# One core, attention and two expert layers: the buffers of the splits, the order of the first loads, and the place of the weight pieces in VectorE's queue

## The chip, the cores and the metric

The kernel runs on one core of a Trainium2 chip. The core has TensorE (PE in the profile, with its weight loads as PEld), VectorE (DVE), ScalarE (ACT), GpSimd (POOL) and SyncE (SP), which issues most of the DMAs. The metric is the device time of one execution in microseconds.

## What is computed

Three layers in a row, on 4 sequences of 576 positions:

```python
# 1: attention, 8 heads of 64, causal by blocks of 64
scores = where(mask, q @ k.T / 8, -1e9)
x = softmax(scores) @ v                       # (4, 576, 512) after joining heads
# 2: a dense layer
xn = (x - mean(x)) / sqrt(var(x) + 1e-6) * g_ln
x = x + relu(xn @ w_ch1) @ w_ch2              # 512 -> 2048 -> 512
# 3: one of 8 experts for each token, chosen by the gate of this token
#    or taken over from the token before
out[b, s] = p[e] * (relu(x[b, s] @ w1[e]) @ w2[e])   # 512 -> 1024 -> 512
```

All inputs are float32; the results are wanted at float32 accuracy.

## The kernel before

**Tiles and steps.** The 2304 tokens are 18 tiles of 128. Attention goes through 144 steps, one for a tile and a head, in the order of the tiles. Matrix products run in float16: each operand is split into a high part and the rest (three matmuls in place of one). A step is: scores (`qk`, PE), row maxima (`maxes`, DVE, L328 and L332), exponentials (`exps`, ACT L339), their split (ACT L348, POOL L351), a transposing DMA issued by SP (L355), and some steps later the product with the values (`pv`, PE L370 and L374).

**Splits of a tile.** Before a tile's steps its keys and queries are cast to float16 (`split_k`, `split_q`: ACT L245 and L230), the rest is subtracted (POOL, for the first tile DVE: L246 and L231), and a transposing DMA brings them into the layout that `qk` reads (SP L247 and L237); DVE makes a copy of the queries with halves exchanged (L238, L239). The values are split without a transpose (`split_v`). A tile's splits are written one tile ahead, at heads `SK`, `SQ` and `SV` of the tile before; its loads are written two tiles ahead.

**End of a tile.** `finish` normalises the attention's result; its normalised rows `xh` are cast, subtracted and transposed (ACT L422, POOL L423, SP L427). `xh`, the keys' `kn` and the queries' `qn` are requests of one ring of three buffers, the tag `nat`, handed out in the order in which the code asks.

**Weights of the dense layer.** They come as 32 pieces of 512 KB (16 of `w_ch1`, 16 of `w_ch2`), read as whole numbers of 64 bits would be and put together again by three DVE passes in `w_bits` (L195, L199, L202; L199 and L202 read two inputs in SBUF). Then ACT scales and casts (`w_hi`: L215, L216) and POOL subtracts (`w_lo`, L220). `w_next` takes one step in this chain: bits of piece p, the high part of p-1 and the load of p+2 (three raw buffers), the rest of p-2. `WPACE[s]` says how many such steps are written at attention step s.

**Dense work.** When a tile (or a group of tiles) is finished, its first layer (16 pieces `l1`, 12 matmuls each, evicted by ACT L477 and DVE L478) and its second layer (4 pieces `l2` a tile, L495 to L497) go into a queue. At each step some are written, as many as a running account allows, and only those whose weights have been written: `need(q) <= wpos - 3`, where `wpos` counts the `w_next` steps so far; a first-layer piece f needs weight piece 4*(f//4)+3, a second-layer piece c needs 16+4*c+3.

**Order.** A scheduler puts the instructions into the engines' queues. It goes by the order of the code, except that instructions written inside `tc.high_priority(HP)` come 400 places earlier; an instruction whose inputs are ready may pass one that is not. `first(i)` gives this precedence to steps of tiles i < `HT`. Everything up to attention step 0 is written in order by hand: `PRE` lists the first loads, `FIRST` the first splits and weight steps (an integer loads that weight piece, "k" loads keys, "K" splits them, "w" is one `w_next`).

**Late buffers.** From step `LATE` on the raw weight buffers are given back, and the rings of scores (`sm`), split exponentials (`ph`) and transposed ones (`pt`) get 1, 2 and 1 more buffers; `pv` then lags 5 steps in place of 4.

Of the kernel before, what the change touches and what calls it, by code (L numbers as in the profile page):

```python
# [10 lines left out]
F16 = mybir.dt.float16  # L11
# [38 lines left out]
LAG = 4  # L50
LATE = 32
MSM = 1
# [8 lines left out]
SK = 3  # L61
# [3 lines left out]
PK = 4  # L65
PRE = (0, "k", "q", 1, "v", 2)
FIRST = ("w", "K", "Q", "w", "V", "w")
RB = 4
ACAP = 20000
FREE = 16  # L70
HP = 400
HT = 2
MAN = 0
# [8 lines left out]
PUMP = (5, 1, 1, 4, 12, 4)  # L82
WPACE = [0]*2+[2]*16


@with_exitstack
def kernel(
# [139 lines left out]
    def split_q(i, eng):  # L227
        r = raw.pop(("q", i))
        n = at.tile([P, H, 2, D], F16, tag="nat", name="qn", bufs=3)
        nc.scalar.copy(out=n[:, :, 0], in_=r)  # L230
        eng.tensor_tensor(out=n[:, :, 1], in0=r, in1=n[:, :, 0], op=ALU.subtract)  # L231
        o = (KRING + VRING + turn_q[0] % 2 * 2) * 1024
        turn_q[0] += 1
        a, b = (
            spare[:, x:x + 1024].rearrange("p (h c) -> p h c", h=H) for x in (o, o + 1024)
        )
        nc.sync.dma_start_transpose(out=a, in_=n.rearrange("p h e d -> p (h e d)"))  # L237
        nc.vector.tensor_copy(b[0:D], a[D:P])  # L238
        nc.vector.tensor_copy(b[D:P], a[0:D])  # L239
        qt[i, 0], qt[i, 1] = a, b  # L240

    def split_k(i, eng):
        r = raw.pop(("k", i))
        n = at.tile([P, H, 2, D], F16, tag="nat", name="kn", bufs=3)
        nc.scalar.copy(out=n[:, :, 0], in_=r)  # L245
# [71 lines left out]
    def maxes(i, h):  # L317
# [7 lines left out]
        if h == 0:  # L325
            sums[i] = at.tile([P, 2, H], F32, tag="sums", name="sums", bufs=2)
        nm = sums[i][:, 0, h:h + 1]
        nc.vector.tensor_tensor_reduce(  # L328
            out=sm[:, lo:n], in0=sp[:, lo:n], in1=mask[:, 5 * P - n + lo:5 * P],
# [62 lines left out]
    def finish(i):  # L392
# [27 lines left out]
        )  # L420
        xh = at.tile([P, 2, DM], F16, tag="nat", name="xh", bufs=3)
        nc.scalar.copy(out=xh[:, 0], in_=xn)  # L422
# [239 lines left out]

    wpos = [0]


    def w_next(n=1):
        for _ in range(n):
            p = wpos[0]
            wpos[0] += 1
            if p < 32:  # L670
                w_bits(p)
# [48 lines left out]
    def first(i):  # L720
        return tc.high_priority(HP) if i < HT else ExitStack()
# [15 lines left out]
    for s in range(nsteps + LAG + MPT):  # L737
# [8 lines left out]
        if s < nsteps:  # L746
# [9 lines left out]
            if t + 1 < NTILE:  # L756
                nx = ORDER[t + 1]
                if h == SK:
                    split_k(nx, nc.gpsimd)
                if h == SQ:  # L760
                    split_q(nx, nc.gpsimd)
                if h == SV:
                    split_v(nx)
                if h == SL:
                    load_tile(t + 2)
# [589 lines left out]
```

## Time and profile before

| | us |
|---|---|
| median of 3 runs | 838.88 |
| lowest, highest | 836.36, 843.30 |
| the profiled execution: its own time | 843.15 |
| the profiled execution: span, first to last instruction | 841.40 |
| PE busy in the span | 707.7 (84%) |
| DVE busy | 460.1 (55%) |
| ACT busy | 362.1 (43%) |
| POOL busy | 327.8 (39%) |
| mean granted TensorE clock | 0.978 |

Busy times are unions of an engine's instructions. In the views below an instruction stands as start (us), duration (us), engine, line, operation, output and inputs, and in square brackets how long its engine had been idle and what ended that. In views by line the count comes first (x16), then busy time, mean duration in ns, and the idle time before. In views by stretch a row gives the stretch, its length, then each engine's busy time with its number of instructions, the clock, the share of the DMA engines' time and their rate.

### The profile page before, as it was taken

The numbers are of one execution on the slowest core, as the hardware profiler recorded it, in microseconds if no ns is written. First come the engines' busy times: TensorE is split into PE (matmuls) and PEld (weight loads), VectorE is DVE, ScalarE is ACT, GpSimd is POOL, SyncE is SP. The second block draws the span as 40 slices with busy tenths as digits, with TensorE's granted clock in tenths as the row PEclk, the third lists the DMA queues.
The fourth block names the chain that finished last, engine by engine and source line by source line (L and its number), as shares of the span: only waits on it lengthen the run. The fifth ranks groups of instructions, "written<-read, shape, count | busy, mean of one in ns | idle before, by whom it ended". The sixth has DMA issues, their size and how long they took to land. (4 is left out here: it accounts for less than half of the span.)

```text
span 841.4 us, 16461 instructions
## 1 busy us (share of the span) xinstructions
PE 707.7 (84%) x5526; PEld 425.4 (51%) x5526; DVE 460.1 (55%) x1248; ACT 362.1 (43%) x843; POOL 327.8 (39%) x364
## 2 busy tenths in 40 slices
PE   0214758789899999898998999998997999999995
PEld 0113645486756857655654565555452444444442
DVE  2999979887755556765564575276881111111110
ACT  2764657675555437555553464164041111111110
POOL 1577747776465235454444553210002122112210
PEclk9999989999999999999999999999998999999999
DMA  9998998799987677799967865397116655665673
GB/s 193 194 227 203 210 203 196 147 184 178 168 144 157 132 141 153 123 184 173 166 131 132 170 100 102 65 341 253 40 43 127 112 125 126 125 121 130 132 129 73
DMA packets 328942, 127.33 MB, mean 151 GB/s; under 512 B 296912, under 2 KB 315344, under 8 KB 328848
## 3 DMA queue, kind: packets, MB, share of 16 engines
q1 hardware_dynamic: 321472, 100.73, 63.0%
q10 hardware_dynamic: 4176, 15.21, 6.8%
q0 software_dynamic: 3200, 10.23, 3.7%
q8 instruction: 48, 0.79, 0.4%
q14 instruction: 46, 0.38, 0.2%
HBM read 128.73 MB, written 9.70 MB: 165 GB/s over the span
## 5 line engine op out<-in xcount | busy, mean ns | idle before, releaser
L473 PE MATMUL dps<-xg,wide 128*128 128x128 f16 (+2 forms) x576 | 156.4, 282 | 28.0 <-DVE htl L478 14.8
L351 POOL TENSOR_TENSOR ph<-sm,ph 128x512 f16<-128x512 f32 (+6 forms) x120 | 132.2, 1105 | 121.8 <-ACT ph L348 83.9
L474 PE MATMUL dps<-xg,wide 128*128 128x128 f16 (+2 forms) x576 | 156.7, 282 | 0.0
L475 PE MATMUL dps<-xg,wide 128*128 128x128 f16 (+2 forms) x576 | 156.6, 282 | 0.0
L339 ACT ACTIVATE sm<-sm,sums 128x128 f32<-128x128 f32 (+8 forms) x144 | 87.9, 611 | 111.5 <-DVE sums L332 100.7
L308 PE MATMUL ps_s<-wide 128*128 128x128 f16 (+4 forms) x560 | 74.9, 260 | 49.2 <-DVE sums L328 27.4
L1001 DVE SCALAR_TENSOR_TENSOR hth<-hps,hth 128x512 f16<-128x512 f32 x38 | 26.2, 691 | 164.6 <-ACT hth L1000 164.4
L495 PE MATMUL dps<-wide,hth 128*128 128x512 f16 x288 | 110.8, 386 | 0.2 <-DVE early L564 0.2
L496 PE MATMUL dps<-wide,hth 128*128 128x512 f16 x288 | 110.7, 385 | 0.0
L497 PE MATMUL dps<-wide,htl 128*128 128x512 f16 x288 | 110.4, 383 | 0.0
L370 PE MATMUL ps_o<-wide,pt 128*128 128x128 f16 x464 | 59.3, 225 | 29.3 <-DVE ob L383 19.0
L474 PEld LDWEIGHTS <-wide 128*128 128x128 f16 x576 | 58.9, 102 | 47.1 <-issue 33.8
L478 DVE SCALAR_TENSOR_TENSOR htl<-dps,hth 128x128 f16<-128x128 f32 (+2 forms) x144 | 59.1, 417 | 42.2 <-ACT hth L477 41.7
L1025 POOL DMA_INDIRECT out<-eo,dst_i x19 | 19.2, 1013 | 156.1 <-ACT eo L1024 151.4
L328 DVE CUSTOM_DVE_ANT_0 sm<-ps_s,mask_a 128x256 f32<-128x256 f32 (+7 forms) x128 | 64.2, 516 | 18.2 <-POOL ph L351 9.6
L308 PEld LDWEIGHTS <-wide 128*128 128x128 f16 x560 | 39.6, 101 | 61.8 <-issue 27.3
L348 ACT CAST ph<-sm 128x512 f16<-128x512 f32 (+6 forms) x120 | 68.2, 570 | 1.6
L477 ACT ACTIVATE hth<-dps 128x128 f16<-128x128 f32 (+2 forms) x144 | 53.5, 375 | 33.5 <-PE dps L475 33.3
L475 PEld LDWEIGHTS <-wide 128*128 128x128 f16 x576 | 59.1, 103 | 14.8
L473 PEld LDWEIGHTS <-wide 128*128 128x128 f16 x576 | 59.1, 103 | 14.6 <-issue 0.6
L370 PEld LDWEIGHTS <-pt 128*128 128x128 f16 x464 | 43.7, 100 | 26.3 <-DMA pt<-ph 17.9
L374 PE MATMUL ps_o<-wide,pt 128*128 128x64 f16 x464 | 55.9, 197 | 0.0
(255 smaller groups left out, 1408.4 us busy)
## 6 DMA issues: line engine op xcount, KB each, us to landing
raws<-in_moe_w SPq DMA_DIRECT2D x38, 2048.0 KB
wraw<-in_moe_w_ch ACTq DMA_DIRECT2D x29, 512.0 KB
raws<-in_moe_w SPq DMA_DIRECT2D x24, 512.0 KB
rows<-x2h SPq DMA_DIRECT2D x18, 256.0 KB
raw<-in_k SPq DMA_DIRECT2D x32, 128.0 KB
raw<-in_q SPq DMA_DIRECT2D x32, 128.0 KB
raw<-in_v SPq DMA_DIRECT2D x32, 128.0 KB
pt<-ph SPq DMA_TRANSPOSE x120
```

What stands on the lines that cost most here:

```text
L308: nc.tensor.matmul(sp[:, a * P + o:b * P], lhsT=qt[i, part].rearrange("p (x t) c -> p x (t c)", t=2)[:, x, z::2], rhs=rhs, start=part == 0 ...
L328: nc.vector.tensor_tensor_reduce(out=sm[:, lo:n], in0=sp[:, lo:n], in1=mask[:, 5 * P - n + lo:5 * P], scale=-0.125, scalar=3.0e38, op0=ALU ...
L339: nc.scalar.activation(out=e, in_=e, func=AF.Exp, scale=-1.0, bias=sv[:, 0, h:h + 1], accum_out=sv[:, 1, h:h + 1],)
L348: nc.scalar.copy(out=ph4[:, :, 0, lo:], in_=sm[:, :, lo:])
L351: nc.gpsimd.tensor_tensor(out=ph4[:, :, 1, lo:], in0=sm[:, :, lo:], in1=ph4[:, :, 0, lo:], op=ALU.subtract)
L370: nc.tensor.matmul(o, lhsT=t[:, c], rhs=vt[kk][:, h].rearrange("p e d -> p (e d)"), start=c == 0, stop=False,)
L473: nc.tensor.matmul(hp, lhsT=wh, rhs=xg[g][:, kk], start=kk == 0, stop=False)
L474: nc.tensor.matmul(hp, lhsT=wh, rhs=xg[g][:, KD + kk], start=False, stop=False)
L475: nc.tensor.matmul(hp, lhsT=wl, rhs=xg[g][:, kk], start=False, stop=kk == KD - 1)
L495: nc.tensor.matmul(op[j], lhsT=hh, rhs=w2h[:, f], start=f == 0, stop=False)
L496: nc.tensor.matmul(op[j], lhsT=hh, rhs=w2l[:, f], start=False, stop=False)
L497: nc.tensor.matmul(op[j], lhsT=hl, rhs=w2h[:, f], start=False, stop=f == KF - 1)
```

## The change

The tag `nat` (3 buffers) is divided: keys and queries keep 2, the normalised rows get one of their own, so the memory stays the same. The first loads are keys, queries, weight piece 0, values; pieces 1 and 2 are loaded behind the first tile's splits of keys and queries, and all three first weight steps stand behind those splits. Weight steps are spread to steps 1, 3, 5, 7 and then one a step up to 34; each step's `w_bits` is queued on DVE behind that step's row maximum (`issue_after` fixes the order in the queue without a wait). `LATE` goes to 40. Precedence holds for tiles 0 to 3 and now for the splits of these tiles too.

```diff
-LATE = 32
+LATE = 40
...
-PRE = (0, "k", "q", 1, "v", 2)
-FIRST = ("w", "K", "Q", "w", "V", "w")
+PRE = ("k", "q", 0, "v")
+FIRST = ("K", "Q", 1, 2, "w", "V", "w", "w")
...
-HT = 2
+HT = 4
...
-WPACE = [0]*2+[2]*16
+WPACE = [0, 1] * 4 + [1] * 27
...
     def split_q(i, eng):
         r = raw.pop(("q", i))
-        n = at.tile([P, H, 2, D], F16, tag="nat", name="qn", bufs=3)
+        n = at.tile([P, H, 2, D], F16, tag="nat", name="qn", bufs=2)
...
     def split_k(i, eng):
         r = raw.pop(("k", i))
-        n = at.tile([P, H, 2, D], F16, tag="nat", name="kn", bufs=3)
+        n = at.tile([P, H, 2, D], F16, tag="nat", name="kn", bufs=2)
...
-        nc.vector.tensor_tensor_reduce(
+        mark["v"] = nc.vector.tensor_tensor_reduce(
             out=sm[:, lo:n], in0=sp[:, lo:n], in1=mask[:, 5 * P - n + lo:5 * P],
...
-        xh = at.tile([P, 2, DM], F16, tag="nat", name="xh", bufs=3)
+        xh = at.tile([P, 2, DM], F16, tag="xh", name="xh", bufs=1)
...
     wpos = [0]
+    mark = {}
...
     def w_next(n=1):
         for _ in range(n):
             p = wpos[0]
             wpos[0] += 1
-            if p < 32:
+            if p < 32 and mark:
+
+                with tc.issue_after(mark["v"].ins):
+                    w_bits(p)
+            elif p < 32:
                 w_bits(p)
...
                 nx = ORDER[t + 1]
-                if h == SK:
-                    split_k(nx, nc.gpsimd)
-                if h == SQ:
-                    split_q(nx, nc.gpsimd)
-                if h == SV:
-                    split_v(nx)
+                with first(nx):
+                    if h == SK:
+                        split_k(nx, nc.gpsimd)
+                    if h == SQ:
+                        split_q(nx, nc.gpsimd)
+                    if h == SV:
+                        split_v(nx)
```

## Rows read from the trace of the kernel before

**Rows 1.** Busy time by stretch: PE, PEld, DVE, ACT, POOL, then clock and DMA.

```profile
0.00:20.00 20.00, 0.39 (x2) 0.13 (x2) 5.13 (x15) 4.58 (x7) 3.56 (x11) 1.00 0.92 189
20.00:52.00 32.00, 7.96 (x50) 5.33 (x51) 31.27 (x83) 22.35 (x57) 18.55 (x16) 1.00 1.00 214
52.00:84.00 32.00, 10.54 (x92) 8.71 (x90) 31.89 (x52) 15.51 (x32) 23.79 (x17) 1.00 0.83 205
84.00:160.00 76.00, 56.34 (x562) 39.39 (x560) 70.34 (x164) 47.60 (x120) 49.18 (x39) 0.93 0.99 197
160.00:202.00 42.00, 36.48 (x464) 27.50 (x462) 31.22 (x110) 30.82 (x86) 31.75 (x37) 0.96 0.98 170
202.00:545.00 343.00, 320.64 (x2864) 211.28 (x2862) 199.19 (x627) 172.40 (x440) 157.42 (x185) 0.99 0.76 141
```

**Rows 2.** DVE by line, 0 to 160 us.

```profile
L202 DVE SCALAR_TENSOR_TENSOR wide<-wraw,wide 128x512 int32<-128x512 int32 x16 | 17.1, 1068 | 0.1
L202 DVE SCALAR_TENSOR_TENSOR wt<-wraw,wt 128x512 int32<-128x512 int32 x16 | 16.1, 1006 | 0.1
L199 DVE SCALAR_TENSOR_TENSOR wt<-wraw,wt 128x512 int32<-128x512 int32 x16 | 15.6, 978 | 0.2
L328 DVE CUSTOM_DVE_ANT_0 sm<-ps_s,mask_a 128x128 f32<-128x128 f32 (+3 forms) x32 | 14.7, 480 | 0.0
L199 DVE SCALAR_TENSOR_TENSOR wide<-wraw,wide 128x512 int32<-128x512 int32 x16 | 13.4, 835 | 0.1
...
L478 DVE SCALAR_TENSOR_TENSOR htl<-dps,hth 128x128 f16<-128x128 f32 x32 | 8.6, 278 | 1.9 <-ACT hth L477 1.9
```

**Rows 3.** All engines in order of time, the first 30 us.

```profile
6.96 0.62 ACT L245 CAST kn<-raw 128x512 f16<-128x512 f32 x1 [4.63 <-DMA raw<-in_k]
...
8.33 2.25 SPq L247 DMA_TRANSPOSE wide<-kn  x1
...
10.68 2.50 SPq L237 DMA_TRANSPOSE wide<-qn  x1
...
18.72 0.43 DVE L195 TENSOR_SCALAR wide<-wraw 128x512 int32<-128x512 int32 x1 [9.81 <-DMA wraw<-in_moe_w_ch]
...
19.47 0.39 PE L308 MATMUL ps_s<-wide 128*128 128x128 f16 x2 [19.47 <-DMA wide<-qn]
...
24.43 1.23 SPq L237 DMA_TRANSPOSE wide<-qn  x1
...
27.20 0.10 PEld L308 LDWEIGHTS <-wide 128*128 128x128 f16 x1 [2.60 <-DMA wide<-qn]
```

**Rows 4.** Line 332, which closes each row maximum, by stretch: busy time and count.

```profile
20.00:52.00 32.00, 1.50 (x14) 1.00 1.00 214
52.00:84.00 32.00, 0.20 (x2) 1.00 0.83 205
84.00:160.00 76.00, 2.48 (x18) 0.93 0.99 197
160.00:202.00 42.00, 2.64 (x19) 0.96 0.98 170
```

**Rows 5.** ACT in order of time, 60 to 72 us.

```profile
62.61 0.62 ACT L422 CAST xh<-xn 128x512 f16<-128x512 f32 x1 [0.20 <-DVE xn L418]
63.14 0.61 ACT L245 CAST kn<-raw 128x512 f16<-128x512 f32 x1
```

**Rows 6.** DMA rate, 0 to 100 us in slices of 2.5 us.

```profile
GB/s 1 250 234 233 246 136 199 210 178 101 140 271 297 162 144 305 236 266 321 224 116 271 243 157 194 224 127 239 191 312 200 249 189 28 238 156 256 194 271 118
```

**Rows 7.** Line 495, the second layer's first matmuls, by stretch: PE, PEld.

```profile
84.00:160.00 76.00, 11.31 (x30) 3.01 (x31) 0.93 0.99 197
```

**Rows 8.** DVE by line, 160 to 202 us.

```profile
L478 DVE SCALAR_TENSOR_TENSOR htl<-dps,hth 128x128 f16<-128x128 f32 x16 | 4.4, 283 | 1.9 <-ACT hth L477 1.9
```

**Rows 9.** Waits, 160 to 202 us: total us, times, longest.

```profile
DVE sm L328 <- POOL ph L351: 3.3, 3, 1.7
```

**Rows 10.** Instructions on the raw weights: duration ns shortest/middle/longest.

```profile
L199 DVE SCALAR_TENSOR_TENSOR wide<-wraw,wide x16: 634/682/1644, 6.2 to 74.5; 128x512 int32<-128x512 int32 x16
```

## The prediction

> **What bounds the kernel now.** I first cut the span into stretches and read each engine's busy time in them [rows 1]. From 202 us on TensorE (PE) is the bound: 320.6 of 343 us up to 545, and the part behind that is not touched at all. Nothing edited here works there, so whatever is won or lost must be won or lost in the first 202 us, where PE is busy for only about 112 us. In 20 to 160 us the busy engine is VectorE (DVE): 31.27 of 32, 31.89 of 32, 70.34 of 76 us. So the second question is what DVE does there. Grouped by line, the conversion of the dense weights leads [rows 2]: the two of its three passes that read two inputs take 17.1, 16.1, 15.6 and 13.4 us, 62.2 of the 138.6 us that DVE works before 160. The bound of the start is DVE, and its biggest customer is the 32 weight pieces.
>
> The third view is the start itself in order of time [rows 3]. SyncE issues weight piece 0, the keys, the queries, piece 1, the values, piece 2, and only then the two transposes; the first score matmul waits until 19.47 us for the transposed queries. DVE stands idle for 9.81 us until 18.72. The fourth view is where the attention steps lie: row maxima per stretch are 14, 2, 18, 19 [rows 4], so 34 of 144 are done by 160, and between 52 and 84 almost none. The reason is in ScalarE's order of time [rows 5]: the third tile's keys are cast at 63.14, directly behind the first tile's normalised rows at 62.61, the previous request of the same three buffers. The ring, not the data, holds the keys.
>
> **The change part by part.** The sum is made against the profiled execution, 843.15 us with a span of 841.40, which lies 4.27 above the median of the three runs, 838.88.
>
> **A, order of the first loads and splits.** Keys and queries go ahead of piece 0, and pieces 1 and 2 are issued behind the two transposes. The keys' cast started at 6.96 behind 512 KB of weights; at the 230 to 250 GB/s of those slices [rows 6] that is 2.2 us, so about 4.8 now. Cast and subtraction took from 6.96 to 8.33, so the keys' transpose is issued at about 6.1. Its issue and that of the queries take 2.25 and 2.50 us as now, or 1.23 each as for the second tile's queries [rows 3]: done between 8.6 and 10.9. From the end of the issue to the landing it is 1.5 us at best (second tile: 25.66 to 27.20) and 6.3 us at worst (now: 13.18 to 19.47). So the first scores can run between 10.1 and 17.2. Now 1,792 KB of loads stand between queries and transposes (pieces 1, 2 and 3 and the values); then 768 KB (piece 0 and the values), 0.43 of it: 6.3 x 0.43 is 2.7, so 11.3 to 13.6. I take 13.0 and A = -6.5 us, bounds -2.3 to -9.4. It reaches DVE, since DVE was idle then; with pieces 1 and 2 landing later, row maxima and the values' split fill the hole.
>
> **B, ring, precedence and pace.** With a buffer of its own the normalised rows no longer hold the third tile's keys, and with precedence for tiles 0 to 3 their row maxima move into the empty stretch of 52 to 84. But DVE was 31.89 of 32 us busy there: maxima that come earlier push weight pieces later, and DVE's work to the 34th step stays the same. Following the counters in the code, the dense pieces written by step 34 are: now the first layer of tiles 0 and 1, the second layer of tile 0 and a quarter of tile 1; then the first layer of tiles 0, 1 and 2 and three quarters of tile 0's second layer, with the last quarter and all of tile 1's at step 34 itself. The trace shows what was really done by 160: 32 first-layer pieces, which is two tiles [rows 2], and 30 of 32 recorded steps of the second [rows 7]. So about equal PE work, but one first layer more ahead of the border: its 16 evictions, 4.4 us of DVE with 1.9 us of waits [rows 8], move from the stretch after 160 into the one where DVE is full. By step 52 both orders have written the same. Before the border that costs up to +4.4; behind it, the stretch of 42 us can shrink to PE's own 36.5 [rows 1], -5.5 at most. Bounds of B together: -5.5 to +4.4; I take -1.5, since the second layer's pieces need no eviction, and PE there can run closer to its own time.
>
> **C, the tie.** Each weight piece traced from step 0 on is queued on DVE behind the row maximum of its step, so behind a maximum that waits for scores or for a free buffer stand its piece, then ScalarE's scaling and GpSimd's (POOL's) subtraction, then the next piece's load. Now row maxima wait 0.0 us on DVE [rows 2], because a piece always fills in. Where no pieces are left they wait 3.3 us on POOL for 19 steps, 0.17 a step [rows 9]. Over 34 steps the bounds are 0 and 6; POOL has slack at 20 to 160 (91.5 of 140 us busy [rows 1]), so I take +1.5.
>
> **D, late buffers from step 40 on instead of 32.** The fifth tile, with the widest maxima, runs with the smaller rings. Lower bound 0; upper twice the 3.3 us that row maxima wait for POOL behind 160, +6.6 [rows 9]. Those steps lie behind the weights' end, where PE has dense work queued: I take +0.5. If that cover is gone the 6.6 is due.
>
> **Costs of nothing.** 32 pieces remain 32 pieces. One buffer for normalised rows is enough because they come once a tile, 19 steps in the 42 us behind 160 [rows 4], so every 18 us or more, and the buffer is held for a cast, a subtraction and a transpose. Two buffers for keys and queries let the next tile's split start when this tile's transposes are through; SyncE's queue carries the transposes of the probabilities behind them, and a transpose of queries that waits there would delay those. PE's other work hides it from 202 us on.
>
> Sum: -6.5 - 1.5 + 1.5 + 0.5 = -6.0, so 837.2 against the profiled execution and 832.9 against the median: **833 us**, a gain below 1%, which is about what a measurement of this kernel can tell from no change.
>
> One price may move on its own. The pieces' two-input passes average 0.97 us (62.2 us by 64) while the shortest takes 0.63, the middle one 0.68 and the longest 1.64 [rows 10], and POOL works beside them. The Trainium skill ("SBUF — State Buffer", section "Who interferes with whom") says that a VectorE instruction with two SBUF inputs and a GpSimd instruction that reads SBUF exclude each other, the second waiting for the end of the first. The spread of these rows agrees with it. By that rule a tie that places each piece at a fixed distance behind a row maximum, and so beside POOL's subtraction for that step, changes the count of meetings. I leave it at zero in the sum.
>
> **The rivals.**
> Faster by over 1%: the early attention lets DVE and PE both stay busy to step 52. Everything is at its good end: A -8, B -5.5, C and D 0, so -13.5 and **825 us**. For it speaks that DVE idles 14.9 us in the first 20 and 10.8 in 160 to 202; against it, that DVE has no slack between.
> Slower, by the tie: in 20 to 160 us a piece may no longer fill DVE's wait for scores. At 0.6 us of waiting a step, 34 steps cost 20 us, which outweighs A and B: -6.5 - 1.5 + 0.5 + 20 = +12.5, **851 us**. It decides from 0.22 us a step on (7.5 / 34), and slower by 1% begins at 0.47 (15.9 / 34). Against it: maxima wait 0.17 a step even where pieces are gone. For it: maxima of 84 to 160 us come only every 4.2 us, and nobody has seen them without filler.
> Slower, by collisions: 30% of the two-input passes collide today if 0.68 is free and 1.64 collided ((0.97 - 0.68) / 0.96). At 50% the 64 passes cost 0.2 x 0.96 x 64, 12 us more: **845 us** with the rest of the sum.
> No effect: DVE's order was already one piece a step on the whole (34 steps and 32 pieces by 160), the tie only writes it down, and DMA, with a share of 0.83 to 1.00 up to 160, hands A back as later weight loads: **839 us**.
>
> **How the numbers follow.** The forecast, 833 with 828 to 838 as its own scatter, has 0.40; a part of 0.08 of it lies just past the 1% (under 830.5). Faster at about 825 has 0.32, no effect 0.15, slower 0.13 (the tie 0.07, collisions 0.06). That gives 0.40 for faster by over 1%, 0.47 for within 1% and 0.13 for slower by over 1%. The range runs from 817 (all good ends, and 8 us of fewer collisions) to 847 (the collision case, and the tie at 0.45 us a step), which leaves out about 2 in 10.
>
> **What would show it.** A: the first score matmul near 13 us and DVE's idle stretch before it 3 to 4 us instead of 9.81. B: the third tile's keys cast by 45 us, row maxima in 52 to 84 us near 8 instead of 2, and the 32nd weight piece near 155. C: an idle time in front of the row maxima above 6 us in 13 to 160 would refute my price; above 16 it makes the kernel slower. D: waits in front of the 640-wide maxima. Collisions: the mean of the two-input passes, 0.97 now. I would be wrong above all if PE's idle time in the first 202 us (90 us) fell by much more than A: then the order of work, not DVE's load, was the bound of the start.

## The result, and the profile after

The changed kernel takes 847.86 us (median of 12 runs, 842.95 to 852.60) against 840.12 (12 runs, 836.36 to 844.78): a ratio of 1.0086, 95% interval [1.0059, 1.0112], 7.2 us slower. The forecast was 833 us, with 817 to 847 as its range. Ratios in this document are taken over executions in the chip's usual state, medians over all of them; in two runs below (loads alone again, without the tie) one to two executions fell into a slower state, so that the median there does not fit the ratio.

One thing has to be said before the traces are laid side by side. The traced execution of after happens to be the shortest of its twelve (842.95, span 841.2), that of before (843.15, span 841.4) is longer than the middle one of its own. The two spans are equal while the medians lie 8 us apart. So stretches are read for the order of work, and for the price a second trace of the same kernel (after again, span 849.9, its own time 851.59 against that kernel's median of 849.15) stands beside it. The page's first part, after and after again:

```profile
PE 708.4 (84%) x5526; PEld 425.5 (51%) x5526; DVE 447.5 (53%) x1248; ACT 363.6 (43%) x843; POOL 330.4 (39%) x364
```

```profile
PE 714.2 (84%) x5526; PEld 428.3 (50%) x5526; DVE 445.6 (52%) x1248; ACT 363.7 (43%) x843; POOL 330.0 (39%) x364
```

Against 707.7 us before, PE has the same 5526 recorded matmuls and is busy 6.5 us longer in the second trace; its idle time (span less busy) is 135.7 against 133.7. Most of what that longer execution lost is matmuls that ran longer, not holes. The mean granted clock points the same way: 0.973 over the runs of before that were timed beside after again, 0.962 over the 12 of after.

All engines in order of time, after, the first 30 us, to be held against [rows 3]:

```profile
4.88 0.62 ACT L245 CAST kn<-raw 128x512 f16<-128x512 f32 x1 [2.55 <-DMA raw<-in_k]
6.25 2.18 SPq L247 DMA_TRANSPOSE wide<-kn  x1
8.53 1.24 SPq L237 DMA_TRANSPOSE wide<-qn  x1
11.46 0.39 PE L308 MATMUL ps_s<-wide 128*128 128x128 f16 x2 [11.46 <-DMA wide<-qn]
18.63 0.62 ACT L245 CAST kn<-raw 128x512 f16<-128x512 f32 x1 [2.95 <-DMA raw<-in_v]
20.56 1.45 SPq L247 DMA_TRANSPOSE wide<-kn  x1
23.32 1.40 SPq L237 DMA_TRANSPOSE wide<-qn  x1
25.70 0.62 ACT L245 CAST kn<-raw 128x512 f16<-128x512 f32 x1 [0.49 <-DMA wide<-kn]
29.13 0.13 PEld L308 LDWEIGHTS <-wide 128*128 128x128 f16 x2 [14.44 <-DMA wide<-qn]
```

The first scores run at 11.46 us, 8.0 earlier than before. The second tile's queries, however, are there only at 29.13, where they were at 27.20 before: PE's wait for them has grown from 2.60 to 14.44 us, most of that because the first tile's scores are done earlier. The third tile's keys are cast at 25.70, where they waited until 63.14 for a buffer of the ring [rows 5].

Busy time by stretch, after (columns as in [rows 1]):

```profile
0.00:20.00 20.00, 2.23 (x16) 1.54 (x16) 8.41 (x31) 5.44 (x10) 3.02 (x11) 1.00 0.86 187
20.00:52.00 32.00, 6.20 (x34) 3.71 (x35) 28.22 (x61) 20.79 (x56) 24.25 (x19) 1.00 1.13 246
52.00:84.00 32.00, 12.11 (x95) 8.02 (x94) 31.73 (x69) 19.77 (x45) 25.16 (x19) 1.00 1.08 210
84.00:160.00 76.00, 54.57 (x667) 42.23 (x667) 72.99 (x166) 49.68 (x126) 50.03 (x40) 0.93 1.09 200
160.00:202.00 42.00, 36.49 (x344) 22.95 (x343) 24.90 (x77) 20.56 (x52) 22.57 (x24) 0.96 0.79 164
```

DVE has worked 8.41 + 28.22 = 36.6 us by 52 us; before it was 5.13 + 31.27 = 36.4. The 3.3 us that it gained in the first stretch are gone in the second, where it now idles 3.8 us. (Such sums are good to about 2 us: two versions below whose edits lie in later steps, late alone and filler in before, have 35.8 and 38.2.) What DVE waited for is not the second tile alone; its longest wait in 20 to 52 us, shown whole where it began earlier, after and then before:

```profile
DVE wg L617 <- DMA wg<-in_moe_w_local: 3.1, 1, 3.1
```

```profile
DVE wide L195 <- DMA wraw<-in_moe_w_ch: 0.6, 2, 0.4
```

L617 scales the weights of the gate, a small load that SyncE now issues at 17.09 us. DVE, early by now, stands before it from 17.76 to 20.90 with the passes of a weight piece queued behind; before, it ran at 26.95 us without a wait. No run moved it alone.

In 160 to 202 DVE, ACT and POOL do much less than before (24.90, 20.56 and 22.57 against 31.22, 30.82 and 31.75) beside the same 36.49 us of PE. Line 332, after, tells what is missing there:

```profile
0.00:20.00 20.00, 0.33 (x4) 1.00 0.86 187
20.00:52.00 32.00, 1.11 (x10) 1.00 1.13 246
52.00:84.00 32.00, 0.90 (x7) 1.00 1.08 210
84.00:160.00 76.00, 2.19 (x16) 0.93 1.09 200
160.00:202.00 42.00, 1.46 (x12) 0.96 0.79 164
```

Added up that makes 14, 21, 37 and 49 row maxima by 52, 84, 160 and 202 us; before it was 14, 16, 34 and 52 [rows 4], since the 34th lies across 160 us and stands in two rows. Attention does come forward, by five steps at 84 us, and has fallen behind by three at 202. What PE does in place of it is line 495, after, to be held against [rows 7] and against the row of 160 to 202 of before, which follows:

```profile
84.00:160.00 76.00, 5.70 (x13) 1.49 (x13) 0.93 1.09 200
160.00:202.00 42.00, 13.38 (x35) 3.45 (x35) 0.96 0.79 164
```

```profile
160.00:202.00 42.00, 6.83 (x18) 1.72 (x18) 0.96 0.98 170
```

The second layer has moved behind 160 us: 35 of its first matmuls in 160 to 202, in place of 18. The stretches from 180 us on, first before, then after:

```profile
180.00:200.00 20.00, 18.78 (x237) 13.78 (x235) 13.26 (x57) 14.14 (x48) 12.27 (x19) 1.00 1.08 176
200.00:206.00 6.00, 5.82 (x72) 4.54 (x71) 5.40 (x13) 1.73 (x5) 4.28 (x7) 1.00 0.78 167
206.00:212.00 6.00, 5.73 (x66) 5.08 (x65) 4.46 (x19) 4.36 (x14) 3.98 (x7) 1.00 0.91 146
```

```profile
180.00:200.00 20.00, 20.00 (x161) 10.91 (x160) 7.36 (x25) 6.17 (x17) 8.05 (x11) 1.00 0.81 175
200.00:206.00 6.00, 2.12 (x26) 1.22 (x24) 4.12 (x8) 3.60 (x11) 2.22 (x3) 1.00 0.51 133
206.00:212.00 6.00, 2.63 (x28) 2.39 (x28) 4.91 (x19) 4.57 (x12) 5.13 (x7) 0.52 0.97 173
212.00:218.00 6.00, 5.03 (x39) 4.08 (x38) 3.79 (x16) 3.91 (x12) 5.20 (x11) 0.63 0.92 189
```

This is the picture to keep. From 180 to 200 PE is never idle, DVE and ACT are at a third: second-layer matmuls stand in PE's queue and the attention steps behind them wait. Then the second layer is used up, the fourth and fifth tile are not finished, and PE is busy 2.12 of 6 us. What it waits for are the attention steps that it held back itself, in the waits of PE, 160 to 226 us, after:

```profile
PE ps_o L370 <- DVE ob L383: 4.9, 3, 3.6
PE ps_s L308 <- DVE sums L328: 4.4, 3, 2.4
```

Part of the way back leads through a load. A product with the values (L370, L374) stands in PE's queue behind the second layer until 193.84; only behind it are the next values split, and SyncE issues the load of the values after those at 196.75. ScalarE waits for it until 201.14, with the exponentials of the row maxima of 197 to 199 us behind it in its queue:

```profile
ACT wide L256 <- DMA raw<-in_v: 5.6, 1, 5.6
```

Behind that hole the granted clock is 0.52 and 0.63, near its lower level of 1.2 GHz, until PE has been busy again. The second trace, after again, shows the same hole some 4 us later, with ScalarE's wait for the values at 5.5 us:

```profile
206.00:212.00 6.00, 0.62 (x8) 0.46 (x8) 5.92 (x17) 4.44 (x14) 4.25 (x5) 0.68 0.59 148
212.00:218.00 6.00, 3.72 (x41) 3.41 (x41) 4.29 (x17) 3.72 (x12) 5.26 (x8) 0.50 1.01 195
```

### The profile page after: what moved, and what is told of

It is laid out like the page before. It is cut to its first block, busy times and chain, and to the rows that moved or that the text cites. A ratio compares the mean times of both kernels' runs of the same rounds, so it can differ in the third digit from the quotient of the medians.

```text
span 841.2 us, 16473 instructions
## 1 busy us (share of the span) xinstructions
PE 708.4 (84%) x5526; PEld 425.5 (51%) x5526; DVE 447.5 (53%) x1248; ACT 363.6 (43%) x843; POOL 330.4 (39%) x364
## 5 line engine op out<-in xcount | busy, mean ns | idle before, releaser
L351 POOL TENSOR_TENSOR ph<-sm,ph 128x512 f16<-128x512 f32 (+6 forms) x120 | 135.2, 1129 | 104.8 <-ACT ph L348 85.3
L308 PE MATMUL ps_s<-wide 128*128 128x128 f16 (+4 forms) x560 | 77.0, 264 | 63.1 <-DVE sums L328 30.4
L478 DVE SCALAR_TENSOR_TENSOR htl<-dps,hth 128x128 f16<-128x128 f32 (+2 forms) x144 | 59.4, 418 | 53.5 <-ACT hth L477 53.3
L370 PE MATMUL ps_o<-wide,pt 128*128 128x128 f16 x464 | 59.9, 226 | 13.0 <-DVE ob L383 6.8
L348 ACT CAST ph<-sm 128x512 f16<-128x512 f32 (+6 forms) x120 | 68.1, 570 | 4.4 <-DMA pt<-ph 3.0
L477 ACT ACTIVATE hth<-dps 128x128 f16<-128x128 f32 (+2 forms) x144 | 53.2, 375 | 31.1 <-PE dps L475 30.8
L374 PE MATMUL ps_o<-wide,pt 128*128 128x64 f16 x464 | 56.4, 199 | 0.0
L1006 ACT ACTIVATE hth<-hps 128x512 f16<-128x512 f32 x38 | 22.6, 596 | 75.4 <-PE hps L989 75.4
## 6 DMA issues: line engine op xcount, KB each, us to landing
raw<-in_k SPq DMA_DIRECT2D x32, 128.0 KB
raw<-in_q SPq DMA_DIRECT2D x32, 128.0 KB
raw<-in_v SPq DMA_DIRECT2D x32, 128.0 KB
```

Of the source, the lines that this page charges most:

```text
L308: nc.tensor.matmul(sp[:, a * P + o:b * P], lhsT=qt[i, part].rearrange("p (x t) c -> p x (t c)", t=2)[:, x, z::2], rhs=rhs, start=part == 0 ...
L348: nc.scalar.copy(out=ph4[:, :, 0, lo:], in_=sm[:, :, lo:])
L351: nc.gpsimd.tensor_tensor(out=ph4[:, :, 1, lo:], in0=sm[:, :, lo:], in1=ph4[:, :, 0, lo:], op=ALU.subtract)
L370: nc.tensor.matmul(o, lhsT=t[:, c], rhs=vt[kk][:, h].rearrange("p e d -> p (e d)"), start=c == 0, stop=False,)
```

## The experiments

All runs were timed beside the kernel before. "Clock" is the mean granted clock over a kernel's runs, beside 0.972 to 0.974 for before, whose median lay between 839.4 and 841.1 from round to round; "idle" is the traced span less PE's busy time; the traced execution can lie some us off the median.

| run | median us | ratio [95%] | clock | span | PE busy | idle |
|---|---|---|---|---|---|---|
| before | 840 | 1 | 0.973 | 841.4 | 707.7 | 133.7 |
| after again | 849.15 | 1.0094 [1.0060, 1.0128] | 0.964 | 849.9 | 714.2 | 135.7 |
| loads alone | 846.99 | 1.0091 [1.0055, 1.0126] | 0.971 | 839.2 | 707.2 | 132.0 |
| loads alone, again | 847.93 | 1.0055 [1.0015, 1.0094] | 0.969 | 848.1 | 710.8 | 137.4 |
| ring alone | 840.23 | 1.0027 [0.9999, 1.0054] | 0.971 | 835.1 | 710.0 | 125.0 |
| pace and late alone | 845.94 | 1.0076 [1.0050, 1.0102] | 0.962 | 840.8 | 710.4 | 130.4 |
| late alone | 844.96 | 1.0061 [1.0031, 1.0091] | 0.968 | 845.7 | 708.4 | 137.3 |
| without the tie | 848.08 | 1.0074 [1.0040, 1.0108] | 0.962 | 851.0 | 716.1 | 134.9 |
| without precedence | 845.61 | 1.0081 [1.0053, 1.0108] | 0.966 | 841.2 | 712.0 | 129.3 |
| old loads | 849.42 | 1.0082 [1.0050, 1.0113] | 0.966 | 844.6 | 711.3 | 133.4 |
| old pace and late | 848.95 | 1.0087 [1.0055, 1.0118] | 0.962 | 849.1 | 718.7 | 130.4 |
| 2nd tile's loads earlier | 852.37 | 1.0138 [1.0083, 1.0193] | 0.960 | 855.1 | 714.9 | 140.3 |
| held loads | 844.16 | 1.0034 [1.0003, 1.0065] | 0.964 | 843.6 | 711.0 | 132.6 |
| held loads, old pace | 845.00 | 1.0049 [1.0020, 1.0078] | 0.963 | 844.9 | 717.0 | 127.9 |
| loads alone, held | 844.71 | 1.0039 [1.0016, 1.0063] | 0.970 | 842.3 | 712.5 | 129.8 |
| filler | 852.00 | 1.0146 [1.0098, 1.0194] | 0.967 | 848.9 | 725.1 | 123.8 |
| filler in before | 850.80 | 1.0116 [1.0082, 1.0151] | 0.973 | 848.8 | 718.4 | 130.4 |
| filler, held loads | 850.09 | 1.0120 [1.0079, 1.0162] | 0.971 | 849.8 | 721.8 | 128.0 |
| held loads, spread | 849.86 | 1.0130 [1.0090, 1.0169] | 0.962 | 849.9 | 714.1 | 135.8 |

**The changed kernel again**, no edit.

> The changed kernel once more, unaltered, for a second trace and the granted clock of more runs. Three theories stand. Order: the weight pieces end later (last piece at 168.6 us against 157.4 in the two traces), so the second layers of the first tiles come late, the 54th attention step is reached at 214.9 instead of 207.9, and the kernel is slower by some 5 to 8 us whatever the clock. Clock: the order of work is worth nothing, but PE is granted a lower clock (0.956 to 0.972 in the twelve runs, 0.978 in the one profiled run of the kernel before), and times follow the clock: about 842 us at 0.972, 848 at 0.960. Later buffers: the loss arises behind 202 us from splits that run further ahead. Order expects the 54th step at about 215 again and the ratio at 1.006 to 1.011; clock expects a trace with less than 0.968 whose extra time lies in low-clock stretches behind 200 us, and a shared kernel before whose runs show 0.97 or more; later buffers expects the same 54th step as before, within 3 us.

1.0094: the loss is there a second time, and 46 row maxima are done by 202 us (49 in the first trace, 52 before), as order expects. Clock as the whole cause falls: where the clocks are alike, 23 runs of before at 0.963 to 0.967 average 842.5 us and six of the 18 of after 847.1. Over the 117 runs of before that were timed beside all these versions, compared within each round, 0.01 of clock goes with some 2.7 us, so the lower clock of after (0.962 for 0.973) goes with about 3 of the 7.2 us, an estimate from these runs; which of the two brings the other they do not say.

**Loads alone**, in the kernel before, twice:

```diff
-PRE = (0, "k", "q", 1, "v", 2)
-FIRST = ("w", "K", "Q", "w", "V", "w")
+PRE = ("k", "q", 0, "v")
+FIRST = ("K", "Q", 1, 2, "w", "V", "w", "w")
```

> The kernel before with the new order of first loads and splits alone. The two traces show the first score matmul at 11.46 instead of 19.47 us, 8 us earlier. My step A: 6.5 us come back at the end, ratio 0.990 to 0.995, if DVE's work from there to the weights' end is what counts. Order: some of it is lost on the way, 0.993 to 1.000. Clock: an earlier start without an end that moves, 0.998 to 1.002 at the same clock.

> The kernel before with the new order of first loads and splits alone, a second time, for its trace in a usual run: the six runs of it so far lie at 840.9 to 851.1, and the one traced was the fastest. Loads theory: ratio 1.005 to 1.012 again, the second tile's queries at 30 us or later. If the first result was chance: 0.998 to 1.003.

1.0091 and 1.0055: the edit that was to bring 6.5 us costs 4.6 to 7.6. Order of time, the second of these runs, SyncE's queue and PE:

```profile
12.20 0.40 PE L308 MATMUL ps_s<-wide 128*128 128x128 f16 x2 [12.20 <-DMA wide<-qn]
19.23 1.26 SPq L169 DMA_DIRECT2D raw<-in_k  x2
21.18 1.68 SPq L247 DMA_TRANSPOSE wide<-kn  x1
22.96 1.28 SPq L169 DMA_DIRECT2D raw<-in_q  x2
24.33 1.28 SPq L237 DMA_TRANSPOSE wide<-qn  x1
34.83 0.61 PE L308 MATMUL ps_s<-wide 128*128 128x256 f16 x2 [19.12 <-DMA wide<-qn]
```

The first tile is early, and its early steps issue the third tile's keys (19.23) ahead of both of the second tile's transposes, and its queries (22.96) ahead of the second of them. The queries' transpose, issued by 25.61, lands at 34.83, 9.2 us later; before it was 1.5 (25.66 to 27.20). DVE's work in 20 to 52 us, 31.27 before, and its longest wait there:

```profile
20.00:52.00 32.00, 5.78 (x32) 3.02 (x32) 22.65 (x56) 18.32 (x50) 18.01 (x15) 1.00 1.10 196
```

```profile
DVE wide L195 <- DMA wraw<-in_moe_w_ch: 7.7, 3, 4.4
```

With the 2.9 us for the gate's weights that is 10.6 us of waiting, where before it had waited 9.81 for a weight piece ahead of 20 us [rows 3]. How this becomes time at the end is less clear: the first loads-alone trace, the fastest of its six executions, has the queries as late (35.42 us) and a span of 839.2.

**Ring alone**, in the kernel before:

```diff
-        n = at.tile([P, H, 2, D], F16, tag="nat", name="qn", bufs=3)
+        n = at.tile([P, H, 2, D], F16, tag="nat", name="qn", bufs=2)
...
-        xh = at.tile([P, 2, DM], F16, tag="nat", name="xh", bufs=3)
+        xh = at.tile([P, 2, DM], F16, tag="xh", name="xh", bufs=1)
```

(`kn` as `qn`.)

> The kernel before with one edit alone: the normalised rows get a buffer of their own, keys and queries share two. Later buffers: this edit carries the loss, ratio 1.006 to 1.011, with the row maxima behind 202 us later than in the kernel before. Order: within 3 us of the kernel before, since weight pieces keep their pace and pass row maxima as before; the third tile's keys are cast by 45 us instead of 63.14. My prediction's step B: no time of its own, 0.997 to 1.003. Clock: goes with the granted clock.

1.0027, an interval that includes no change. Its trace casts the third tile's keys at 30.77 us and has 21 row maxima by 84: the ring alone brings the attention forward, without a gain and without a price that can be told.

**Without the tie**, in the changed kernel:

```diff
-            if p < 32 and mark:
-
-                with tc.issue_after(mark["v"].ins):
-                    w_bits(p)
-            elif p < 32:
+            if p < 32:
                 w_bits(p)
```

> The changed kernel without the tie: weight pieces may again pass row maxima on DVE, all else as changed. Order, with the tie as its cause: the last weight piece comes at 155 to 160 us instead of 168.6, and 4 to 8 us come back (ratio 0.998 to 1.004). Order, with the pace as its cause: nothing comes back (1.006 to 1.011), last piece still at 165 or later. Clock: no more than 2 us either way, unless the granted clock moves with it. Later buffers: nothing comes back.

1.0074 beside 1.0086 and 1.0094: the tie costs nothing that can be told from the runs, and the weight pieces' last pass does not come earlier (174.71 us, 168.57 with the tie).

**Old loads**, in the changed kernel: the loads' edit above backwards.

> The changed kernel with the old order of first loads and splits; ring, tie, pace, late buffers and precedence as changed. The theory now: the new order brings the first scores 8 us forward (11.46 for 19.47), but the second tile's queries land later (29.1 in the changed kernel, 31.9 with the new order alone, 27.2 before), PE stands 14 to 20 us before them, and the DMAs of weight pieces and of the third tile that were let in ahead cost more than the early start gives. It expects this kernel at 0.998 to 1.003 of the one before. The rival, pace: the loss of the changed kernel comes from the weight pieces' late end (168.6 for 157.4) which pace and precedence bring; it expects 1.006 to 1.011 here, and the 54th step near 215.

1.0082, as the rival expected, and the hole is there again (PE busy 1.22 of 6 us in 206 to 212). The part that costs 0.6 to 0.9% alone gives nothing back when it is taken out of the whole.

**The second tile's loads earlier**, in the changed kernel, ahead of weight pieces 1 and 2:

```diff
-FIRST = ("K", "Q", 1, 2, "w", "V", "w", "w")
+FIRST = ("K", "Q", "L", 1, 2, "w", "V", "w", "w")
...
+        elif what == "L":
+            for nm in "kqv":
+                load_x(ORDER[1], nm, nc.sync)
...
-T1 = 1
+T1 = -1
```

> The changed kernel with the second tile's loads issued ahead of weight pieces 1 and 2 (they were issued behind them). If the second tile's late data costs the gain, its queries land at 25 us or earlier, DVE works 30 us or more of the 32 between 20 and 52, and 4 to 8 us come back (0.998 to 1.004). If the pieces' late end costs it, it gets worse, since pieces 1 and 2 come 3 us later still: 1.009 to 1.014.

1.0138. The second tile's queries are there at 28.35 in its trace, no more than 0.8 earlier, and DVE is busy 20.25 of the 32 us of 20 to 52: it waits 6.0 us for these queries and 3.2 for weight pieces. Their transpose was issued by 20.21, ahead of every load of the third tile, and landed 8.1 us later. So the third tile's loads are not all that can delay it; what did here, with the DMA share at 1.11, was not isolated.

**Held loads**, in the changed kernel: the third tile's loads are queued on SyncE behind the transpose of the second tile's queries.

```diff
-        nc.sync.dma_start_transpose(out=a, in_=n.rearrange("p h e d -> p (h e d)"))
+        late["t"] = nc.sync.dma_start_transpose(out=a, in_=n.rearrange("p h e d -> p (h e d)"))
...
-                if h == SL:
+                if h == SL and t == 0:
+                    with tc.issue_after(late["t"].ins):
+                        load_tile(2)
+                elif h == SL:
                     load_tile(t + 2)
```

> The changed kernel with the third tile's loads queued on SyncE behind the transpose of the second tile's queries (in the trace before they stood behind it, in the changed one the keys are issued at 18.60, ahead of both transposes at 20.56 and 23.32). If what hurts is that these loads take the DMA engines ahead of the transposes, the queries land at 27 us or earlier and 2 to 6 us come back (1.001 to 1.006). If it is the weights' end, nothing: 1.006 to 1.011.

1.0034 [1.0003, 1.0065], by its middle value the best of all versions with an early start. Its queries land at 30.06, though (29.13 without the hold): it does not win by them. What its trace changes is 20 to 52 us, where DVE is busy 30.08 us in place of 28.22 and the DMA share is 1.03 in place of 1.13.

**The pace.** Four runs: the old pace with the old step of the late buffers in the changed kernel, the changed kernel without the precedence, new pace and late buffers alone in the kernel before, and held loads with the old pace.

```diff
-LATE = 40
+LATE = 32
...
-WPACE = [0, 1] * 4 + [1] * 27
+WPACE = [0]*2+[2]*16
```

> The changed kernel with the old pace of weight steps and the old step 32 for the late buffers; loads, ring, precedence and tie stay as changed. Theory (the new pace uses up the second-layer work before the fourth and fifth tile's group is ready, PE is left empty near 206 us and then runs 10 us at the lower clock): the hole and the low stretch near 206 go, step 54 comes at 208 to 212 us as before, and only the cost of the load order is left, 1.004 to 1.008 of before. Rival (the load order sets it all, the pace nothing): 1.0086 as the whole change. Rival (the precedence makes the hole): the hole stays and the time is 1.007 to 1.010.

> The changed kernel without the precedence of tiles 2 and 3 and of the splits. Theory of the pace: hole near 206 us, its low clock and 1.007 to 1.010 stay. Rival (precedence pushes the weight pieces back, and that makes the last of them start at 168 in place of 157): the last piece starts near 158, the hole is gone, 1.003 to 1.006.

> The kernel before with the new pace and the late buffers from step 40 alone. Theory of the pace: step 54 comes at 215 to 222 us in place of 208, a stretch of low clock lies near 206 to 216, and the time is 1.006 to 1.010 with the old load order. Rival (pace costs only beside precedence and ring, which bring the attention forward): 1.000 to 1.003, no hole.

> The changed kernel with the old pace and step 32, and with the third tile's loads queued on SyncE behind the transpose of the second tile's queries; so both suspected costs are taken out and the early start, the ring, the precedence and the tie are left. If the two costs explain the loss, 0.994 to 1.000 of before: the head start of 8 us is kept in part. If the head start is lost to the DMA rate whatever the order, 1.000 to 1.004.

The theory that the new pace makes the hole and the hole the loss falls: with the old pace the hole near 206 goes (PE busy 5.97 of 6 us in 200 to 206), and the time stays at 1.0087. That would suit the rival by which the load order sets it all, but old loads gave 1.0082. A stretch of the trace with the old pace:

```profile
160.00:180.00 20.00, 10.57 (x64) 5.77 (x63) 13.83 (x36) 12.10 (x23) 13.57 (x12) 0.66 0.51 101
```

The hole is now at 160 to 180, PE 10.57 of 20 at a clock of 0.66. The precedence makes no difference (1.0081), and this run settles one more thing: without it the weight pieces' last pass starts at 157.43, where it was before (157.41), and the hole and the loss stay. So the loss does not need the pieces' late end. The pace and the late buffers alone give 1.0076, the time that was expected of the pace, with a low stretch near 206 (clock 0.50 in 200 to 206); but the late attention that was to go with it is not there (51 row maxima by 202, 52 before). By the middle values the late buffers are most of it, as the last run below shows. Held loads with the old pace give 1.0049, above both ranges that were expected and no better than with the new pace; its PE has the second lowest idle time of the runs without filler (127.9) and one of the longest busy times (717.0).

**Filler.** Does the lower clock behind the hole cost the time, or does it only go with late steps? Fifty matmuls that nobody needs, in the changed kernel, in the kernel before, and with the held loads:

```diff
+        if 46 <= s < 56:
+            fp = ps_d.tile([P, 512], F32, tag="d", name="fps", bufs=3)
+            for n in range(5):
+                nc.tensor.matmul(
+                    fp, lhsT=w1h[:, 0, 0:P], rhs=w1h[:, 0, 0:512], start=n == 0, stop=n == 4
+                )
```

> The changed kernel with five dummy matmuls of 512 columns written in each of the steps 46 to 55; they write a buffer of the dense ring that nobody reads, so the results stay. They are 50 matmuls, some 11 us of PE at the full clock, and the hole of the changed kernel between 200 and 218 us is about 8 us. If the low clock behind the hole costs the time, the stretch of 10.2 us at the lower clock goes and the time is 1.002 to 1.007 of before. If the hole comes from late attention steps and the clock is only its trace, the dummies add work: 1.009 to 1.020.

> The kernel before with the same dummy matmuls, as the price of the filler itself where PE has no hole (5.8 of 6 us busy near 206): all 11 us on the path would be 1.013; with half of them in idle places of 212 to 260 us 1.005. If it is not slower at all, the filler is free everywhere and the changed kernel with it can be read directly.

> The changed kernel with the third tile's loads held behind the transpose of the second tile's queries, and with the dummy matmuls. The hold alone gave 1.0034 with 14 us more of low clock than before, worth 7 us. If the clock of the stretch near 205 is what is left, 0.995 to 1.001; if not, 1.003 to 1.015.

With the held loads and the filler the clock of 200 to 218 us is 1.00:

```profile
200.00:206.00 6.00, 4.59 (x35) 2.40 (x33) 4.08 (x10) 2.85 (x7) 3.35 (x5) 1.00 0.93 187
206.00:212.00 6.00, 4.60 (x50) 3.07 (x48) 4.02 (x17) 4.53 (x14) 3.88 (x8) 1.00 0.91 170
212.00:218.00 6.00, 6.00 (x60) 4.52 (x58) 2.40 (x9) 2.59 (x8) 3.29 (x6) 1.00 0.90 138
```

So a busier PE does keep the clock there. In the changed kernel without the hold a low stretch stays:

```profile
212.00:218.00 6.00, 3.94 (x16) 2.37 (x17) 0.42 (x1) 3.55 (x9) 4.50 (x7) 0.58 0.93 186
```

Both times (1.0146, 1.0120) lie in the ranges expected if the clock is not what costs, but the first is no test of that, since its low stretch stayed; and the filler's price is 9.7 us in before, 5.0 more than without it in the changed kernel (0.0146 - 0.0086 of 840), 7.2 with the held loads (0.0120 - 0.0034). If the three are compared, the hole and its clock are worth some 2.5 to 5 us, and with intervals of 3 to 4 us on each ratio that is not settled.

**Loads alone, held**: the loads' edit and the hold, in the kernel before.

> The kernel before with the new load order and the held loads, old pace, ring, precedence and no tie. If the load order alone (1.0055 to 1.0091) loses because the third tile's loads stand ahead of the second tile's transposes, the second tile's queries land at 26 to 30 us in place of 35, and the time is 0.994 to 1.002, with the clock of before. If it loses because the DMA engines are full in 20 to 52 us whatever the order, 1.004 to 1.008.

Order of time:

```profile
24.27 1.23 SPq L239 DMA_TRANSPOSE wide<-qn  x1
27.05 0.10 PEld L310 LDWEIGHTS <-wide 128*128 128x128 f16 x1 [11.38 <-DMA wide<-qn]
28.41 1.33 SPq L169 DMA_DIRECT2D raw<-in_k  x2
```

The queries land at 27.05 in place of 34.83, 1.6 us after their issue, as expected: in this kernel it is the third tile's loads that delay them. The time, 1.0039, lies under both runs without the hold (1.0055, 1.0091), with overlapping intervals, and it is no gain: the 0.994 to 1.002 that was to follow did not. The second tile is where it was before (27.20), so the 7 us of the first tile are still lost; from 17 us on DVE still waits 3.9 us for weight pieces and 2.9 for the gate's weights.

**Held loads, spread**: the changed kernel with held loads, and the due step of the dense work of tiles 1 and 2 eight steps later.

```diff
-else FS if g < FG
+else FS + 8 * (g in (1, 2)) if g < FG
```

> The changed kernel with the held loads (1.0034 alone), and with the due step of the dense work of tiles 1 and 2 eight steps later, so that second-layer pieces are left for steps 46 to 61, where PE ran empty. If the order of dense work makes the hole, PE's idle time in 160 to 226 us falls from 11 to about 8 us, the stretch of 10.2 us at the lower clock near 205 goes, and the time is 0.996 to 1.001. If the attention steps themselves are late there, the hole stays: 1.002 to 1.006.

1.0130: refuted, and above both ranges. The hole stays, and the lower clock with it:

```profile
200.00:206.00 6.00, 1.26 (x14) 1.20 (x14) 5.67 (x19) 4.69 (x14) 3.48 (x6) 0.58 1.01 201
```

**Late alone**: `LATE = 40` in the kernel before, nothing else.

> The kernel before with the late buffers from step 40 in place of 32, nothing else. If the smaller rings cost nothing there, 0.998 to 1.002, as the prediction had it (0.5 us). If they hold up the steps 32 to 40 (bound 6.6 us), 1.004 to 1.008, and then they are most of what the new pace with late buffers cost (1.0076).

1.0061 [1.0031, 1.0091], 5.1 us. Stretch and waits of its trace, 160 to 226 us:

```profile
160.00:226.00 66.00, 52.21 (x633) 40.97 (x631) 44.99 (x153) 41.21 (x114) 43.30 (x52) 0.93 0.85 160
```

```profile
DVE sm L328 <- POOL ph L351: 4.3, 3, 2.5
DVE sm L328 <- POOL ph L350: 2.6, 1, 2.6
```

and the same stretch before:

```profile
160.00:226.00 66.00, 58.18 (x717) 46.95 (x716) 50.01 (x165) 45.27 (x125) 45.09 (x57) 0.97 0.95 167
```

Row maxima wait 6.9 us for POOL, where it was 3.3 (all of it in [rows 9]), and PE is idle 13.8 us in place of 7.8; PE's longest waits there are for DVE's evictions of the first layer (L478), 6.1 us in place of 2.0. `LATE` also sets from which step on the product with the values lags by five; the two effects were not separated.

## Why the prediction was wrong, step by step

**A, the step that failed: "It reaches DVE, since DVE was idle then; with pieces 1 and 2 landing later, row maxima and the values' split fill the hole."** The landing was right and even too careful: 11.46 us for 13.0, and DVE's idle stretch before it is 3.12 us in place of 9.81. It did reach DVE in the first 20 us. But the sum took a gain at the first tile for a gain at the end of the start. The step was never followed to what DVE needs next: the second tile's data, the weight pieces and the gate's weights, which still came through DMA engines that the trace of before had shown at a share of 0.92 and 1.00 [rows 1]. The second tile's keys are cast at 18.63, 7 us behind the first scores, and DVE stands 3.1 us for the gate's weights. By 52 us it had done the same work as before, within the 2 us of such sums, and PE's idle time in the first 202 us is 90.4 us for 90.3: A was worth about zero there. Alone it was worse, +4.6 to +7.6 us for -6.5, and by 52 us DVE had done 31.1 us of work for 36.4. Part of that is shown: a first tile that is early issues the third tile's loads early, on the queue that carries the second tile's transposes, and holding them brings those queries from 34.83 to 27.05 in the kernel before. That this returns time is likely but not shown: the ratios go from 1.0055 and 1.0091 to 1.0039, with intervals that overlap. In the whole the hold gives 1.0034 for 1.0086 without bringing the queries earlier, so for another reason, which is open. The prediction looked at what stands between the first tile's queries and its transposes; the loads that the first tile's steps issue were moved too, and were not followed.

**D, mis-sized.** The mechanism stands as written (maxima that wait for POOL in smaller rings), as far as it can be told from the later lag, and the bounds of 0 to 6.6 hold the 5.1 us measured alone. The value taken was 0.5, on the ground that "PE has dense work queued" there. PE's idle time in 160 to 226 us rose by 6.0 us. The cover was read from busy time; that the dense work behind it is finite, and that a held-up attention step holds up the next first layer, was not asked. That this is also its price inside the whole change was not shown: the run with the old step and the old pace regained nothing.

**B, right in its order and wrong behind 160 us.** The ring and the precedence did to the order what was said: the third tile's keys at 25.70 ("by 45"), 7 row maxima in 52 to 84 ("near 8"); the ring alone does as much. The 32nd piece was to end near 155 and its last pass starts at 168.57. The ring alone is within 1.0027, and taking the precedence out changes nothing. What failed is the view behind 160 us, that the stretch "can shrink to PE's own 36.5": PE's own time is 36.49 again, but as second-layer work that stood ahead of attention, whose steps on DVE and ACT then come too late. Equal PE work is not equal progress.

**C.** Taken at 1.5 us; no difference can be told, and row maxima wait 1.0 us in the first 160. The rival "slower, by the tie" is out: without the tie next to nothing comes back of the 20 us that it was to cost.

**The collisions.** The two-input passes on the raw weights average 1.064 us after (68.1 us by 64) against 0.97: 5.9 us more of DVE, half of what the rival had assumed. Loads alone (62.2) and late alone (61.5) lose their time without them, and in the changed kernel with the old pace they are back at 61.6 while the time stays at 1.0087. So the rival does not carry the loss. Its 845 us lay nearest to what was measured, by luck. The Trainium skill ("SBUF — State Buffer", section "Who interferes with whom") has the exclusion that would make such passes longer; the spread is there again, 1.49 us beside 0.68 among the last four passes of line 202, but no run here varied POOL's work alone.

**No effect** was the rival nearest in its mechanism. Its clause that DMA hands A back as later weight loads fits (with the loads alone, 7.7 us of waits for weight pieces behind 20 us, 0.6 before); that the rest would then be zero did not.

**The sum.** It added parts, and the parts do not add. Loads alone (+4.6 to +7.6) and pace with late (+6.4, of which late alone makes +5.1) come to more than the 7.2 us of the whole, and neither old loads nor old pace and late in the changed kernel give any back. What the versions share is in the table: the early or re-paced ones show lower clocks (0.960 to 0.966 in the changed family without filler, 0.962 in pace and late alone), and in most of their traces PE is busy longer at the same matmuls, behind a hole near 170 or near 206; the loads alone and the late buffers alone lose more by idle time in their traces (137.4 and 137.3 for 133.7). That the clock is the common cause is argued from the table, and it can't be all: at like clocks after is still 4.6 us slower, and the loads alone lose their time at 0.969 to 0.971. The filler shows that the clock can be kept up in one place, not that this pays. What stays open is why each new order has such a hole, and a version that beats both kernels was not found: only the ring alone can't be told from the kernel before, all others are slower. An intermediate step for the late buffers with the held loads was not tried, nor a later place for the gate's weights in DVE's queue.

## What to carry to other kernels

A head start is worth what is left of it at the next thing that is waited for: follow it to the second tile, to the loads that an earlier first tile issues and to every instruction that stands next in the busy engine's queue, and look whether the DMA engines have room for them. Where two streams share PE, count the progress of the slower one by its steps (here the row maxima by stretch), since PE's busy time stays the same when it does the wrong one first. And where a price hangs on a cover (here 0 to 6.6 us), ask how much of the cover is left at that place before taking the lower end.

## What the runs showed of the hardware that was not expected

The granted clock falls behind holes: in after it stood at 1.00 through 20 us in which PE was busy without a break, and fell to 0.52 behind a stretch of 6 us with 2.12 busy; with the filler in that place, held loads, it stayed at 1.00. A transposing DMA issued behind 256 KB loads on the same queue took 9.2 us to land, and 1.6 us when those loads were held back; but one that stood ahead of them took 8.1 us in another version (the second tile's loads earlier), so their place is not all that counts. Two traces of one kernel can differ by 1% in span (841.2 and 849.9 us, after and after again).
